# Another order around the second batch's attention, and v cast by ScalarE

## Chip, core and metric

The kernel runs on one core of a Trainium2 chip. The time is the device time of one launch in microseconds, lower is better. Batches and tiles are counted from 0 throughout, as in the code: "batch 1" is the second one.

## What is computed

Linear attention with cosine weights over 8 batches, 8 heads, 576 positions and 64 elements per head, and then a two-layer network with a leaky ReLU over the 4608 rows of 512 that it gives:

```python
def phi(x, c, s):
    r = np.maximum(x, 0.0)
    return np.concatenate([r * c, r * s], axis=-1)   # 64 -> 128
q_p, k_p = phi(q, cos_w, sin_w), phi(k, cos_w, sin_w)
kv  = np.einsum('bhsf,bhsd->bhfd', k_p, v)           # sum over positions
z   = np.sum(k_p, axis=2)
num = np.einsum('bhsf,bhfd->bhsd', q_p, kv)
den = np.einsum('bhsf,bhf->bhs', q_p, z)[..., None] + 1e-06
x   = (num / den)  # rows: batch and position, columns: head and element
h   = x @ w_in                                       # 512 -> 2048
out = np.maximum(0.01 * h, h) @ w_out                # 2048 -> 512
```

## The kernel before

**Tiling.** Of each batch's 576 positions 512 are its main part (four tiles of 128, j = 0 to 3) and 64 its tail. The tails of k and v join their own batch's sums (`kpt`, `vtail`); the tails of q of all batches form a ninth group of 512 rows, so that the network runs over 9 groups g of 512 rows each. Everything is cast to 16-bit floats before TensorE takes it, sums are in 32 bits in PSUM.

**Stages of a batch.** Loads of q, k and v (SyncE's queue; one pool `stage` of 7 buffers of 1 MB, handed out in order). `q_prep` and `k_main`/`k_tail` make phi on VectorE (some cosine halves on ScalarE). `v_main` and `v_tail` cast v. `kv_mm` does 4 x 9 matmuls for the sums over positions, with two columns of ones beside v, so that z comes along; `kv_all`, or `kv_half` for four heads, copies them out of PSUM on ScalarE. phi(q) is transposed, by TensorE for batches 0 and 1, by DMA from batch 2 on (`q_transpose_dma`). `num` (or `num_half`) multiplies by kv, `divide` on VectorE does den, its reciprocal and the product. The result is transposed to xT: TensorE and a copy by ScalarE for batches 0 to 2, DMA after that.

**The network.** `ffn1(g, m)` is a unit of four matmuls of 512 columns for one block m of 128 hidden features (16 of them); two blocks share a PSUM tile `h`, which ScalarE's Lrelu turns into `g`. `ffn2(g, i)` is a unit of four matmuls of the second product: tile i // 4 of 128 rows, a quarter of the hidden features each; the fourth unit of a tile is followed by the copy of `ps_o` to `osb` and the output DMA.

**PSUM.** 8 banks in three pools: "h" two tiles of two banks, "o" two tiles of one bank, "n" one tile of two banks. Each pool hands out its tiles in turn, so an allocation waits for the last reader of the tile that it takes over.

**Order.** It is written out by hand; each engine runs its instructions in the order of the program and waits on semaphores. Batch 1's attention stands between the last units of group 0's second product: this stretch runs at about 44 to 56 us of the profile. Behind it, a list of units (f1 and f2 alternating, 16 positions to a group) is woven with the steps of the later batches: each step has a position, and goes in front of the first unit whose position isn't smaller. `load_steps(b, pk, pv, pq)` gives the positions of the loads of k, v and q, `kv_steps(b, start, step, mm, eng_v)` those of phi(k), of v's casts (`start + 3 * step`) by engine `eng_v`, and of `kv_all` (`mm`); `q_steps(b, start, step, lag)` those of phi(q) and, `lag` later, of its transposition. All DMAs, loads, transpositions and outputs alike, are issued from SyncE's one queue in this order.

**The functions and lines that matter here:** L260 and L270 are the matmuls of `kv_mm`, L282 and L287 its copies, L368 and L333 those of num, L385 the transposes, L389 and L612 the copies to xT, L411 and L430 the two products, L419 the Lrelu, L228 and L230 the casts and copies (`copy`: ScalarE, and the other engines), L222 phi on VectorE, L86 and L96 the loads of main parts and tails, L304 and L315 the DMA transpositions, L446 the outputs.

Of the kernel before, what the change touches and what calls it, by code (L numbers as in the profile page):

```python
# [9 lines left out]
dt = mybir.dt  # L10
# [3 lines left out]
P = 128  # L14
J = 4
# [3 lines left out]
def kernel(  # L19
# [14 lines left out]
    nc = tc.nc  # L34
# [11 lines left out]
    NE = D + 2  # L46
# [3 lines left out]
    def pool(name, bufs, space=None):  # L50
        kw = {"space": space} if space is not None else {}
        return ctx.enter_context(tc.tile_pool(name=name, bufs=bufs, **kw))
# [16 lines left out]
    ps_o = pool("ps_o", 2, PS)  # L69
    ps_n = pool("ps_n", 1, PS)  # L70

    def psum(where, shape, dtype, name):
        p = {"h": ps_h, "o": ps_o, "n": ps_n}[where]
        return p.tile(shape, dtype, name=name, tag="ps_" + where)

    st = {}
    ACT, DVE, POOL = nc.scalar, nc.vector, nc.gpsimd
# [81 lines left out]
    def idle(n):  # L159
# [21 lines left out]
        base=0,  # L181
# [3 lines left out]
    for o in range(2):  # L185
# [3 lines left out]
            base=MAIN,  # L189
# [24 lines left out]
    kv = [const.tile([P, H, NE], dt.float16, name=f"kv{b}") for b in range(B)]  # L214
# [3 lines left out]
    def phi_half(eng, o, i, col):  # L218
        if eng is ACT:
            nc.scalar.activation(o, i, AF.Relu, scale=col)  # L220
        else:
            eng.tensor_scalar(  # L222
                out=o, in0=i, scalar1=0.0, scalar2=col, op0=ALU.max, op1=ALU.mult
            )
# [11 lines left out]
    def k_main(b, j, eng_c, eng_s, lo=0, hi=H):  # L236
        kpm, kst = st["kpm", b], st["k", b]
        for eng, t, f in ((eng_c, cos_t, 0), (eng_s, sin_t, D)):
            phi_half(
                eng, kpm[:, lo:hi, j, f : f + D], kst[:, lo:hi, j, :], t[:, j : j + 1]  # L240
            )
# [6 lines left out]
    def v_main(b, lo, hi, eng):  # L248
        copy(eng, vmain[b % 2][:, lo:hi, :, 0:D], st["v", b][:, lo:hi])
# [6 lines left out]
    def kv_mm(b, hg, ps):  # L256
        kpm, kpt = st["kpm", b], st["kpt", b]
        for cc in range(2):
            c = 2 * hg + cc
            nc.tensor.matmul(  # L260
                ps[:, 2 * cc * NE : 2 * (cc + 1) * NE],
                lhsT=kpt[:, c, :],
                rhs=vtail[b % 2][:, c].rearrange("p a e -> p (a e)"),
                start=True,
                stop=False,
            )
            for o in range(2):
                h = 2 * c + o
                for j in range(J):
                    nc.tensor.matmul(  # L270
                        ps[:, (2 * cc + o) * NE : (2 * cc + o + 1) * NE],
                        lhsT=kpm[:, h, j, :],
                        rhs=vmain[b % 2][:, h, j, :],
                        start=False,
                        stop=(o == 1 and j == J - 1),
                    )
# [4 lines left out]
            kv_mm(b, hg, ps[:, hg])  # L281
        nc.scalar.copy(kv[b].rearrange("p (a h) e -> p a (h e)", a=2), ps)  # L282

    def kv_half(b, hg, where):
        ps = psum(where, [P, 4 * NE], dt.float32, "ps_kvh")
        kv_mm(b, hg, ps)
        nc.scalar.copy(kv[b][:, 4 * hg : 4 * hg + 4].rearrange("p h e -> p (h e)"), ps)  # L287

    def q_src(g, j):
        if g < B:  # L290
# [84 lines left out]
    def x_transpose_half(g, jp, hg, ps=None, out=True):  # L375

        if ("xT", g) not in st:
            st["xT", g] = xtpool.tile([P, NKC, MAIN], dt.float16, name="xT")
        xp = st["xp", g, jp]
        if ps is None:  # L380
            ps = psum("o", [P, 2, 2 * P], dt.float16, "ps_xth")
        for cc in range(2):
            for o in range(2):
                h = 4 * hg + 2 * cc
                nc.tensor.transpose(  # L385
                    ps[:, cc, o * P : (o + 1) * P], xp[:, o, h : h + 2, :], ident
                )
        if out:
            nc.scalar.copy(  # L389
                st["xT", g][:, 2 * hg : 2 * hg + 2, jp * 2 * P : (jp + 1) * 2 * P], ps  # L390
            )
# [10 lines left out]
    def ffn1(g, m, lo=0, hi=MAIN, chunks=range(NKC), where="h"):  # L402

        if ("g", g) not in st:
            st["g", g] = gpool.tile([P, NFT, MAIN], dt.float16, name="g")
        if m % 2 == 0 and chunks[0] == 0 and lo == 0:
            st["h", m // 2] = psum(where, [P, 2, MAIN], dt.float32, "ps_h")
        xT = st["xT", g]
        ps = st["h", m // 2]
        for c in chunks:  # L410
            nc.tensor.matmul(  # L411
                ps[:, m % 2, lo:hi],
                lhsT=w1[m // 4][c // 2][:, c % 2, m % 4 : 512 : 4],
                rhs=xT[:, c, lo:hi],
                start=(c == 0 and lo == 0),
                stop=(c == NKC - 1 and hi == MAIN),
            )
        if m % 2 == 1 and chunks[-1] == NKC - 1 and hi == MAIN:
            nc.scalar.activation(st["g", g][:, m - 1 : m + 1, :], ps, AF.Lrelu)  # L419

    def ffn2(g, i, eng=DVE):
        tt, part = divmod(i, 4)
        if g == NG - 1 and tt == 3:
            last_tile(*divmod(part, 2))
            return
        if part == 0 and ("ps_o", g, tt) not in st:
            st["ps_o", g, tt] = psum("o", [P, DM], dt.float32, "ps_o")
        ps = st["ps_o", g, tt]
        for m in range(4 * part, 4 * part + 4):
            nc.tensor.matmul(  # L430
                ps,
                lhsT=st["g", g][:, m, tt * P : (tt + 1) * P],
                rhs=w2[:, m, :],
                start=(m == 0),
                stop=(m == NFT - 1),
            )
        if part == 3 and eng is not None:
            ffn2_out(g, tt, eng)

    def ffn2_out(g, tt, eng):  # L440
        ps = st["ps_o", g, tt]
        osb = opool.tile([P, DM], dt.float32, name="osb", tag="osb")
        if g < B:
            copy(eng, osb, ps)
            rows = out[g * S : g * S + MAIN, :].rearrange("(p j) d -> p j d", j=J)
            nc.sync.dma_start(rows[:, tt, :], osb)  # L446
            return
        copy(eng, osb, ps)
        for o in range(2):
            r0 = (2 * tt + o) * S + MAIN  # L450
            nc.sync.dma_start(out[r0 : r0 + TAIL, :], osb[o * TAIL : (o + 1) * TAIL, :])
# [100 lines left out]
            u()  # L552
        assert not steps

    def f1(g, m):
        return lambda: ffn1(g, m)

    def f2(g, i):
        return lambda: ffn2(g, i)
# [21 lines left out]
    ps = psum("n", [P, 2, DM], dt.float32, "ps_o")  # L581
# [11 lines left out]
        ffn2(0, 4 * tt + 3, None)  # L593
    ffn2_out(0, 2, DVE)
    ffn2_out(0, 3, DVE)
    kv_half(1, 0, "h")
    for j in range(J):
        k_main(1, j, ACT if j < 3 else DVE, DVE, 4, 8)
    v_main(1, 4, 6, POOL)
    v_main(1, 6, 8, ACT)  # L600
    ffn2(0, 2)
    num_half(1, 0, 0, "h")
    num_half(1, 1, 0, "n")
    ffn2(0, 4 + 2)
    kv_half(1, 1, "h")
    ffn2(0, 3, ACT)
    num_half(1, 0, 1, "h")
    num_half(1, 1, 1, "h")
    ps = psum("n", [P, 2, MAIN], dt.float16, "ps_x")
    for jp in range(2):  # L610
        x_transpose_half(1, jp, 0, ps[:, :, jp * 2 * P : (jp + 1) * 2 * P], False)
    nc.scalar.copy(st["xT", 1][:, 0:2, :], ps)  # L612
    ffn2(0, 4 + 3, ACT)
    for m in range(2):
        ffn1(1, m, 0, MAIN, range(0, 2))
    x_transpose_half(1, 0, 1)
    x_transpose_half(1, 1, 1, psum("n", [P, 2, 2 * P], dt.float16, "ps_xth"))
    for m in range(2, 4):
        ffn1(1, m, 0, MAIN, range(0, 2))
    for m in range(4):  # L620
# [3 lines left out]

    units = []
    for m in range(4, NFT):
        units.append((8 + m / 2, f1(1, m)))
    for g in range(1, NG):
        ahead = {1: 8, 2: 4}.get(g, 0)
        order = [f2(g, i) for i in range(ahead)]  # L630
# [10 lines left out]
    def kv_steps(b, start, step, mm, eng_v, n_act=0):  # L641
        at(start - 0.01, kp_tiles, b)
        at(start, k_tail, b, DVE, DVE)
        for i in range(J):
            at(start + (i + 1) * step, k_main, b, i, ACT if i < n_act else DVE, DVE)
        at(start + 3 * step, v_main, b, 0, 4, eng_v)
        at(start + 3 * step + 0.1, v_main, b, 4, 8, eng_v)
        at(start + 3 * step + 0.2, v_tail, b, eng_v)
        at(mm, kv_all, b)

    def load_steps(b, pk, pv, pq):
        at(pk, load_k, b)
        at(pv, load_v, b)
        at(pq, load_main, "q", q, b)
# [6 lines left out]
    def q_steps(b, start, step, lag):  # L661
        for j in range(J):
            at(start + j * step, q_prep, b, j)
            at(start + j * step + lag, q_transpose_dma, b, j)
# [9 lines left out]
    kv_steps(3, 20, 0.7, 24, ACT)  # L674
    out_steps(3, 24.5, 1.4, 1)

    load_steps(4, 20.5, 22.5, 19)
    kv_steps(4, 28, 1.2, 34, POOL)
    q_steps(4, 30, 1, 0.8)
    out_steps(4, 36.8, 2, 1.6)  # L680

    for b in range(5, NG):
        base = 16 * (b - 2)
        if b < B:
            load_steps(b, base - 14.5, base - 13, base - 17)
            kv_steps(b, base - 9.5, 1.4, base - 2, POOL)
        else:
            for j in range(J):
                at(base - 11.5 + 2 * j, load_qtail, j)
        q_steps(b, base - 8, 2, 1)  # L690
        out_steps(b, base + 1, 2, 1.6)
# [32 lines left out]
```

## Time and profile before

| what | value |
|---|---|
| median of 3 runs | 298.75 us (296.34, 298.75, 429.62) |
| profiled execution | 297.1 us, span 295.0 us |
| TensorE busy in the span | 286.8 us (97%) |
| VectorE, ScalarE, GpSimd busy | 132.9, 107.8, 24.0 us |
| granted TensorE clock, mean | 1.000 |
| matmuls of the two products | 592 + 560 instructions |
| DMA moved | 56.93 MB |

The span runs from the first to the last instruction that the profiler saw; the time includes what lies around it. Starts are in microseconds from the span's start. In a row of the timeline the first number is the start, the second the duration of what is merged in the row, and a bracket tells how long the engine had been idle and who released it. PE is TensorE, DVE VectorE, ACT ScalarE, POOL GpSimd, SPq the instruction queue of SyncE. The matmuls are pipelined and their ends are modelled, so that two rows overlap where TensorE is full, and the distance between starts tells more than the durations.

### The profile page before, as it was taken

How to read it: one execution, taken by the hardware profiler on the slowest of the kernel's cores; microseconds unless marked ns; L12 is line 12 of the kernel's file. 1: busy time of each engine (PE TensorE's matmuls, PEld its weight loads, DVE VectorE, ACT ScalarE, POOL GpSimd, SP SyncE). 2: the span in 40 equal slices, each digit the busy share in tenths (PEclk: the TensorE clock that was granted, in tenths of full speed). 3: DMA queues.
4: the chain of work that ended last, by engine and by line, in shares of the span. 5: the costliest groups of instructions: out<-in, count | busy, mean ns of one | idle time of the engine just before them, and what ended most of it. 6: DMA issues, size and time to landing. Idle time of an engine off the chain costs nothing.

```text
span 295.0 us, 4811 instructions
## 1 busy us (share of the span) xinstructions
PE 286.8 (97%) x1932; PEld 153.9 (52%) x1932; DVE 132.9 (45%) x328; ACT 107.8 (37%) x128; POOL 24.0 (8%) x36
## 2 busy tenths in 40 slices
PE   8799999999999999999999999999999999999995
PEld 3575556465455455555545554555445544444444
DVE  6950578934855925933572347333323211000011
ACT  4846376664253422242223222322222232222200
POOL 2055000000000400400300021000000000000000
PEclk9999999999999999999999999999999999999999
DMA  7999999999999999999978995416681210011132
GB/s 219 355 386 406 290 350 346 329 170 333 186 269 285 205 248 265 267 158 315 241 143 230 216 234 126 110 53 144 143 159 56 71 53 38 36 43 61 41 71 71
DMA packets 88773, 56.93 MB, mean 193 GB/s; under 512 B 56880, under 2 KB 81712, under 8 KB 88240
## 3 DMA queue, kind: packets, MB, share of 16 engines
q1 hardware_dynamic: 88672, 56.57, 75.7%
q8 instruction: 15, 0.25, 0.4%
q14 instruction: 6, 0.05, 0.1%
q10 hardware_dynamic: 80, 0.07, 0.1%
HBM read 36.70 MB, written 9.44 MB: 156 GB/s over the span
## 4 chain that ended last, share of the span: by engine, by line
PE 80%; DMA 13%; SPq 3%; ACT 1%; issue 0%; DVE 0%; POOL 0%
PE ps_h L411 37%; PE ps_o L430 37%; DMA ktl<-in_k_dram 5%; DMA w1st<-in_moe_w_in_dram 4%; DMA vst<-in_v_dram 3%; PE ps_num L333 3%; PE ps_kv L270 2%; SPq L86 2%; SPq L96 1%; SPq L138 1%; DMA out_dram<-osb 1%; PE ps_kv L260 0%; ACT xT L389 0%; ACT g L419 0%; ACT xT L612 0%
## 5 line engine op out<-in xcount | busy, mean ns | idle before, releaser
L411 PE MATMUL ps_h<-xT,w 128*128 128x512 f16 (+1 forms) x592 | 143.1, 373 | 0.6 <-ACT g L419 0.2
L430 PE MATMUL ps_o<-w,g 128*128 128x512 f16 x560 | 139.4, 379 | 0.0
L419 ACT ACTIVATE g<-ps_h 128x1024 f16<-128x1024 f32 x72 | 73.5, 1024 | 141.7 <-PE ps_h L411 141.6
L411 PEld LDWEIGHTS <-w 128*128 128x128 f16 x592 | 64.3, 114 | 53.6 <-issue 1.3
L430 PEld LDWEIGHTS <-g 128*128 128x128 f16 x560 | 54.1, 98 | 61.6 <-issue 0.2
L230 DVE COPY osb<-ps_o 128x512 f32<-128x512 f32 x33 | 22.7, 690 | 76.6 <-PE ps_o L430 76.6
L344 DVE TENSOR_SCALAR den<-ps_num 128x8 f32<-128x8 f32 x28 | 4.6, 166 | 54.1 <-PE ps_num L333 54.1
L230 POOL CAST vmain<-vst 128x1024 f16<-128x1024 f32 (+1 forms) x9 | 9.8, 1107 | 136.6 <-DMA vst<-in_v_dram 136.6
L349 DVE TENSOR_TENSOR xs<-ps_num,rden 128x512 f16<-128x512 f32 x28 | 19.4, 691 | 1.0
L222 DVE TENSOR_SCALAR kpm<-kst,sin_t 128x512 f16<-128x512 f32 (+1 forms) x40 | 18.3, 472 | 0.7 <-DMA kst<-in_k_dram 0.7
L222 DVE TENSOR_SCALAR qp<-qst,cos_t 128x512 f16<-128x512 f32 (+1 forms) x34 | 16.3, 479 | 3.8 <-DMA qst<-in_q_dram 3.8
L222 DVE TENSOR_SCALAR qp<-qst,sin_t 128x512 f16<-128x512 f32 (+1 forms) x34 | 16.1, 472 | 0.0
L333 PEld LDWEIGHTS <-qpT 128*128 128x128 f16 (+1 forms) x256 | 11.2, 101 | 7.3 <-issue 1.9
L222 DVE TENSOR_SCALAR kpm<-kst,cos_t 128x512 f16<-128x512 f32 (+1 forms) x29 | 14.1, 485 | 0.1
L333 PE MATMUL ps_num<-kv,qpT 128*128 128x66 f16 (+1 forms) x256 | 12.4, 194 | 0.0
L270 PEld LDWEIGHTS <-kpm 128*128 128x128 f16 x256 | 10.6, 97 | 2.8 <-DVE kpm L222 0.7
L162 PE MATMUL ps_idle<-blank 128*128 128x512 f16 x28 | 9.2, 467 | 1.2 <-DVE blank L157 1.2
L228 ACT COPY qpT<-ps_qt 128x1024 f16<-128x1024 f16 x8 | 7.8, 1019 | 7.0 <-PE ps_qt L323 7.0
L230 DVE CAST w<-w2st 128x2048 f16<-128x2048 f32 x4 | 4.9, 1227 | 11.7 <-DMA w2st<-in_moe_w_out_dram 11.7
L230 POOL CAST w<-w1st 128x1024 f16<-128x1024 f32 x8 | 8.3, 1042 | 16.4 <-DMA w1st<-in_moe_w_in_dram 16.4
L270 PE MATMUL ps_kv<-vmain,kpm 128*128 128x66 f16 x192 | 8.1, 193 | 0.0
L348 DVE RECIPROCAL rden<-den 128x8 f32<-128x8 f32 x36 | 7.3, 203 | 1.2
(57 smaller groups left out, 102.6 us busy)
## 6 DMA issues: line engine op xcount, KB each, us to landing
out_dram<-osb SPq DMA_DIRECT2D x32, 256.0 KB, 2.7
qst<-in_q_dram SPq DMA_DIRECT2D x7, 1024.0 KB, 8.0
kst<-in_k_dram SPq DMA_DIRECT2D x6, 1024.0 KB, 7.9
vst<-in_v_dram SPq DMA_DIRECT2D x6, 1024.0 KB, 8.3
w1st<-in_moe_w_in_dram SPq DMA_DIRECT2D x8, 512.0 KB, 12.1
w2st<-in_moe_w_out_dram SPq DMA_DIRECT2D x4, 1024.0 KB, 11.3
kst<-in_k_dram SPq DMA_DIRECT2D x4, 512.0 KB, 8.2
vst<-in_v_dram SPq DMA_DIRECT2D x4, 512.0 KB, 8.6
```

Of the source, the lines that this page charges most:

```text
L86: nc.sync.dma_start(st[nm, b][:, lo:hi], src[b, lo:hi, 0:MAIN, :].rearrange("h (p j) d -> p h j d", j=J),)
L162: nc.tensor.matmul(ps, lhsT=blank[:, 0:P], rhs=blank)
L222: eng.tensor_scalar(out=o, in0=i, scalar1=0.0, scalar2=col, op0=ALU.max, op1=ALU.mult)
L228: nc.scalar.copy(o, i)
L230: eng.tensor_copy(o, i)
L270: nc.tensor.matmul(ps[:, (2 * cc + o) * NE : (2 * cc + o + 1) * NE], lhsT=kpm[:, h, j, :], rhs=vmain[b % 2][:, h, j, :], start=False, stop ...
L333: nc.tensor.matmul(ps[lo:hi, h // 4, (h % 4) * NE : (h % 4 + 1) * NE], lhsT=qpT[:, h, lo:hi], rhs=kv[b][:, h, :],)
L348: nc.vector.reciprocal(rden, den)
L349: nc.vector.tensor_tensor(out=xs, in0=ps[:, :, 0 : 4 * NE].rearrange("p a (b e) -> p a b e", e=NE)[:, :, :, 0:D], in1=rden.rearrange("p (a ...
L411: nc.tensor.matmul(ps[:, m % 2, lo:hi], lhsT=w1[m // 4][c // 2][:, c % 2, m % 4 : 512 : 4], rhs=xT[:, c, lo:hi], start=(c == 0 and lo == 0 ...
L419: nc.scalar.activation(st["g", g][:, m - 1 : m + 1, :], ps, AF.Lrelu)
L430: nc.tensor.matmul(ps, lhsT=st["g", g][:, m, tt * P : (tt + 1) * P], rhs=w2[:, m, :], start=(m == 0), stop=(m == NFT - 1),)
```

## The change

Between the last units of group 0's second product and the first units of group 1, the same work is put in another order: `ffn2(0, 2)` goes ahead of `kv_half(1, 0)`, whose copy now follows the first pair of phi(k) casts; `ffn2(0, 6)` and `ffn2(0, 3)` go ahead of where they were; the last unit of tile (0, 1) is split into two pairs of matmuls (`ffn2_mm`), one ahead of the second num pair and one behind the first transposes. The output copy of tile (0, 0) follows `kv_half(1, 1)`, that of tile (0, 1) goes to VectorE. The two last transposes share a PSUM tile of pool "o" and stand on either side of the first `ffn1` units; h of m = 4 and 5 goes to pool "n". For batches 4 to 7 v is cast by ScalarE instead of GpSimd, q is loaded just ahead of k, for batch 4 k is loaded somewhat later too, and phi(q) of batch 4 is spaced by 0.8 positions instead of 1.

```diff
--- before.py
+++ after.py
@@ -281,10 +281,16 @@
             kv_mm(b, hg, ps[:, hg])
         nc.scalar.copy(kv[b].rearrange("p (a h) e -> p a (h e)", a=2), ps)
 
-    def kv_half(b, hg, where):
-        ps = psum(where, [P, 4 * NE], dt.float32, "ps_kvh")
-        kv_mm(b, hg, ps)
-        nc.scalar.copy(kv[b][:, 4 * hg : 4 * hg + 4].rearrange("p h e -> p (h e)"), ps)
+    def kv_half(b, hg, where, out=True):
+        st["kvh", hg] = psum(where, [P, 4 * NE], dt.float32, "ps_kvh")
+        kv_mm(b, hg, st["kvh", hg])
+        if out:
+            kv_half_out(b, hg)
+
+    def kv_half_out(b, hg):
+        nc.scalar.copy(
+            kv[b][:, 4 * hg : 4 * hg + 4].rearrange("p h e -> p (h e)"), st["kvh", hg]
+        )
 
     def q_src(g, j):
         if g < B:
@@ -425,17 +431,19 @@
             return
         if part == 0 and ("ps_o", g, tt) not in st:
             st["ps_o", g, tt] = psum("o", [P, DM], dt.float32, "ps_o")
-        ps = st["ps_o", g, tt]
-        for m in range(4 * part, 4 * part + 4):
+        ffn2_mm(g, tt, 4 * part, 4 * part + 4)
+        if part == 3 and eng is not None:
+            ffn2_out(g, tt, eng)
+
+    def ffn2_mm(g, tt, lo, hi):
+        for m in range(lo, hi):
             nc.tensor.matmul(
-                ps,
+                st["ps_o", g, tt],
                 lhsT=st["g", g][:, m, tt * P : (tt + 1) * P],
                 rhs=w2[:, m, :],
                 start=(m == 0),
                 stop=(m == NFT - 1),
             )
-        if part == 3 and eng is not None:
-            ffn2_out(g, tt, eng)
 
     def ffn2_out(g, tt, eng):
         ps = st["ps_o", g, tt]
@@ -552,8 +560,8 @@
             u()
         assert not steps
 
-    def f1(g, m):
-        return lambda: ffn1(g, m)
+    def f1(g, m, where="h"):
+        return lambda: ffn1(g, m, where=where)
 
     def f2(g, i):
         return lambda: ffn2(g, i)
@@ -593,28 +601,34 @@
         ffn2(0, 4 * tt + 3, None)
     ffn2_out(0, 2, DVE)
     ffn2_out(0, 3, DVE)
-    kv_half(1, 0, "h")
-    for j in range(J):
+    ffn2(0, 2)
+    kv_half(1, 0, "h", False)
+    k_main(1, 0, ACT, DVE, 4, 8)
+    kv_half_out(1, 0)
+    for j in range(1, J):
         k_main(1, j, ACT if j < 3 else DVE, DVE, 4, 8)
     v_main(1, 4, 6, POOL)
     v_main(1, 6, 8, ACT)
-    ffn2(0, 2)
+    ffn2(0, 4 + 2)
     num_half(1, 0, 0, "h")
     num_half(1, 1, 0, "n")
-    ffn2(0, 4 + 2)
+    ffn2(0, 3, None)
     kv_half(1, 1, "h")
-    ffn2(0, 3, ACT)
+    ffn2_out(0, 0, ACT)
+    ffn2_mm(0, 1, 12, 14)
     num_half(1, 0, 1, "h")
     num_half(1, 1, 1, "h")
     ps = psum("n", [P, 2, MAIN], dt.float16, "ps_x")
     for jp in range(2):
         x_transpose_half(1, jp, 0, ps[:, :, jp * 2 * P : (jp + 1) * 2 * P], False)
     nc.scalar.copy(st["xT", 1][:, 0:2, :], ps)
-    ffn2(0, 4 + 3, ACT)
+    ffn2_mm(0, 1, 14, 16)
+    ffn2_out(0, 1, DVE)
+    ps = psum("o", [P, 2, 2, 2 * P], dt.float16, "ps_x1")
+    x_transpose_half(1, 0, 1, ps[:, 0])
     for m in range(2):
         ffn1(1, m, 0, MAIN, range(0, 2))
-    x_transpose_half(1, 0, 1)
-    x_transpose_half(1, 1, 1, psum("n", [P, 2, 2 * P], dt.float16, "ps_xth"))
+    x_transpose_half(1, 1, 1, ps[:, 1])
     for m in range(2, 4):
         ffn1(1, m, 0, MAIN, range(0, 2))
     for m in range(4):
@@ -624,7 +638,7 @@
 
     units = []
     for m in range(4, NFT):
-        units.append((8 + m / 2, f1(1, m)))
+        units.append((8 + m / 2, f1(1, m, "n" if m < 6 else "h")))
     for g in range(1, NG):
         ahead = {1: 8, 2: 4}.get(g, 0)
         order = [f2(g, i) for i in range(ahead)]
@@ -674,16 +688,16 @@
     kv_steps(3, 20, 0.7, 24, ACT)
     out_steps(3, 24.5, 1.4, 1)
 
-    load_steps(4, 20.5, 22.5, 19)
-    kv_steps(4, 28, 1.2, 34, POOL)
-    q_steps(4, 30, 1, 0.8)
+    load_steps(4, 21.4, 22.5, 21.3)
+    kv_steps(4, 28, 1.2, 34, ACT)
+    q_steps(4, 30, 0.8, 0.8)
     out_steps(4, 36.8, 2, 1.6)
 
     for b in range(5, NG):
         base = 16 * (b - 2)
         if b < B:
-            load_steps(b, base - 14.5, base - 13, base - 17)
-            kv_steps(b, base - 9.5, 1.4, base - 2, POOL)
+            load_steps(b, base - 14.5, base - 13, base - 14.6)
+            kv_steps(b, base - 9.5, 1.4, base - 2, ACT)
         else:
             for j in range(J):
                 at(base - 11.5 + 2 * j, load_qtail, j)
```

## Prediction

> **What bounds the kernel now.** I read the page first, then the waits, then TensorE's timeline where it is not full, then the other engines around each place that the change touches. Batches are counted from 0, so "batch 1" is the second and "batch 4" the first whose v cast changes engine.
>
> ```profile
> span 295.0 us, 4811 instructions
> PE 286.8 (97%) x1932; PEld 153.9 (52%) x1932; DVE 132.9 (45%) x328; ACT 107.8 (37%) x128; POOL 24.0 (8%) x36
> PEclk9999999999999999999999999999999999999999
> ```
>
> TensorE has work nearly throughout, at full granted clock. The busy share alone would hide small bubbles, since ends of matmuls are modelled, so I take starts: four 512-column matmuls in a row take 0.86 us wherever nothing waits (0.86 x4 all along the chain that ended last). What is over that is lost. TensorE's timeline:
>
> ```profile
> 44.40 0.22 PE L260 MATMUL ps_kvh<-vtail,kpt 128*128 128x132 f16 x1
> 44.90 0.41 PE L270 MATMUL ps_kvh<-vmain,kpm 128*128 128x66 f16 x8 [0.28 <-DVE vmain L230]
> ...
> 47.70 0.22 PE L260 MATMUL ps_kvh<-vtail,kpt 128*128 128x132 f16 x1
> 48.13 0.58 PE L270 MATMUL ps_kvh<-vmain,kpm 128*128 128x66 f16 x8 [0.21 <-POOL vmain L230]
> ...
> 50.68 1.03 PE L430 MATMUL ps_o<-w,g 128*128 128x512 f16 x4
> 51.94 1.02 PE L411 MATMUL ps_h<-xT,w 128*128 128x512 f16 x4 [0.24 <-ACT xT L612]
> ...
> 53.25 2.99 PE L411 MATMUL ps_h<-xT,w 128*128 128x512 f16 x12
> 56.48 5.34 PE L411 MATMUL ps_h<-xT,w 128*128 128x512 f16 x24 [0.25 <-ACT g L419]
> ```
>
> A 132-column start is followed 0.06 us later by the next elsewhere: 0.44 lost at 44.40, 0.37 at 47.70; the eight short matmuls at 48.13 need 0.42 to the next group instead of 0.26, so 0.16 more. 50.68 + 0.86 = 51.54, the next starts 51.94: 0.40. 53.25 + 12 x 0.216 = 55.84, the next starts 56.48: 0.64 (0.24 inside the row, 0.41 behind it). Together **2.0 us**. From 56.48 to the last matmuls I find only about 0.75 us more, around 221 to 234, in the tail group that the change leaves alone. So all that the reorder can win is 2.0 us of 297; two per cent, about what a measurement of this kernel can tell from no change, is 6 us.
>
> **The change, part by part.** The order of batch 1, followed from 44.40:
>
> - ffn2(0, 2) goes ahead of kv_half(1, 0): TensorE reaches kv at 44.40 + 0.86 = 45.26, VectorE's v cast ends 44.85 and ScalarE's 45.13. The 0.44 is covered. ScalarE now casts cosine of j = 0 ahead of kv's copy; that cast can't start before k's second half lands (45.94 now). So 45.94 + 0.44, then 0.38 for the copy: 46.76. TensorE is there at 45.26 + 0.63 + 0.86 = 46.75; with 0.05 for the signal (51.89 to 51.94 above) it loses 0.06.
> - ffn2(0, 3) goes ahead of kv_half(1, 1): num takes 0.51, ffn2 0.86, so kv starts at 48.18. POOL's cast ends 47.46 + 0.62 = 48.08, ScalarE's at about 48.2 and is needed only by the second half. The 0.37 and 0.16 are covered.
> - Between kv_half(1, 1) and num there are now two matmuls (0.43) where there were four. kv ends 48.81, its copy starts 0.22 later and takes 0.38; num can start at 49.45, TensorE is there at 49.24. A **new wait of 0.21**, and up to 0.16 for starting short matmuls again (as at 48.13): 0.1.
> - The other two matmuls and half a transposition now cover the 1.01 us copy of xT. Four heads' transposes end 50.47; the copy runs about 50.67 to 51.68. But x_transpose_half(1, 0, 1) needs VectorE's division: den at about 49.95, then 0.17, 0.20, 0.69 with their gaps, 51.08. TensorE is there at 50.90 and loses 0.3; after 0.22 of transposing it is at 51.43 and waits 0.3 for xT, where it waited 0.40.
> - The last transposition stands alone, so its copy (0.55) ends at about 53.55, before the chunks that need it (53.68): the 0.24 is gone. h of m = 4 and 5 goes to the bank pair "n", free since 51.68: the 0.41 is gone.
>
> Sum: -2.01 + 0.06 + 0.21 + 0.1 + 0.3 + 0.3 = **-1.0** (between -2.0, no new wait, and +0.5, each new wait three times as long with the old ones gone).
>
> What is late next: the output copy of (0, 1) moves from ScalarE to VectorE, which issues one each 0.64 us (1.28 for the two at 44.76) and has no idle time from 50.17 to 60.25. It starts 0.17 earlier, so batch 2's last kpm comes at 60.25 + 0.47 = 60.72, and TensorE comes to kv_all(2) at 61.66 - 1.04 = 60.62, needing that piece four weight loads later. I take **+0.2** (0 to 0.5).
>
> **v on ScalarE** from batch 4. The nearest rows are batch 3, which already has it:
>
> ```profile
> 79.76 1.02 ACT L419 ACTIVATE g<-ps_h 128x1024 f16<-128x1024 f32 x1 [4.65 <-PE ps_h L411]
> 80.68 1.98 ACT L228 CAST vmain<-vst 128x1024 f16<-128x1024 f32 x2
> 82.57 0.83 ACT L228 CAST vtail<-vtl 64x256 f16<-64x256 f32 x2
> 83.42 1.03 ACT L419 ACTIVATE g<-ps_h 128x1024 f16<-128x1024 f32 x1
> ```
>
> From the start of g to the end of the last v cast: 83.40 - 79.76 = 3.64. For batch 4 the casts' positions (31.6 to 31.8) lie behind the last f1 unit of batch 2 (31.5), so they follow its g, and only four f2 units lie between that and kv_all(4):
>
> ```profile
> 100.10 1.03 ACT L419 ACTIVATE g<-ps_h 128x1024 f16<-128x1024 f32 x1 [0.70 <-PE ps_h L411]
> 102.96 0.48 DVE L222 TENSOR_SCALAR kpm<-kst,sin_t 128x512 f16<-128x512 f32 x1
> 103.36 0.22 PE L260 MATMUL ps_kv<-vtail,kpt 128*128 128x132 f16 x1
> ```
>
> 100.10 + 3.64 + 0.05 = 103.79 against 103.36: TensorE waits 0.43, whatever the shift before it, since both follow the same f1. With a slow restart **+0.5** (0 to 1.0). Behind the casts stand kv's copy and the next g; for batches 5 to 7 kv_all comes three positions (over 5 us) later, and a g held 0.4 us is needed only some 4 us on: nothing. By "TensorE: Matmul & The Clock Gate" (the Trainium skill, on the array's architecture) ScalarE and VectorE take their queues strictly in order, so that these casts can't step aside; the row at 83.42, a g starting just as v's cast ends, agrees, and an engine that could reorder would give 0 in place of 0.5.
>
> POOL's casts are gone, and with them this:
>
> ```profile
> 97.16 2.55 POOL L230 CAST vmain<-vst 128x1024 f16<-128x1024 f32 x2 [49.08 <-DMA vst<-in_v_dram]
> 97.55 1.26 DVE L222 TENSOR_SCALAR kpm<-kst,cos_t 128x512 f16<-128x512 f32 x1
> 98.73 1.25 DVE L222 TENSOR_SCALAR kpm<-kst,sin_t 128x512 f16<-128x512 f32 x1
> ```
>
> Two casts of 1.26 instead of 0.48 and two of 0.6: 1.9 us less on VectorE. Without that, kpm of batch 4 (103.44 at its end, against TensorE's load at 103.36) would hold TensorE the moment it comes earlier. Eight pairs of 0.79 from 95.1 end at 101.4, TensorE comes at 102.5: 1.1 us of cover. "SBUF — State Buffer" (the Trainium skill, on who interferes with whom) says that VectorE in a two-port mode and GpSimd lock each other out for a whole instruction; the 1.26 beside a cast of 1.27 agrees, and by it the gain here is full.
>
> **Loads.** q of batch 4 goes from position 19 to 21.3, k from 20.5 to 21.4: behind all four transpositions of qp of batch 3 (18.8 to 21.2), not among them. SyncE's queue now:
>
> ```profile
> 77.60 0.52 SPq L86 DMA_DIRECT2D qst<-in_q_dram  x1
> 79.27 6.76 SPq L304 DMA_TRANSPOSE qpT<-qp  x2
> 86.08 0.57 SPq L86 DMA_DIRECT2D kst<-in_k_dram  x1
> 90.80 0.59 SPq L86 DMA_DIRECT2D vst<-in_v_dram  x1
> ```
>
> The transpositions took 2.5 to 3.5 each behind 1 MB of q; elsewhere 1.25. Three at 1.25 from about 78.2 put q and k at 82 to 83, k no later than its 86.08, landing 7.9 later (median) plus about 3 for the q ahead of it: 93. VectorE wants it at 92.9. At 3.3 each, q goes at 88 and k lands near 99. I take 0 (0 to +4.4). qp's transposes come sooner, which the last num of batch 3 needs. For batches 5 to 7 q goes just ahead of k; for batch 5 VectorE already waits 2.67 us for ktl (at 115.33) and TensorE loses nothing by it.
>
> **Sum**: -1.0 + 0.2 + 0.5 + 0 = -0.3. The profiled execution took 297.1 (span 295.0): **296.8**. The median shown, 298.75, is of runs at 296.34, 298.75 and one far off; 297.1 lies between the two near ones, so execution noise (2.4 us) is larger than the whole effect.
>
> **Rivals.** (1) The casts of batch 4 cost nothing and the reorder holds: 297.1 - 0.8 = 296.3. Against it stands the 3.64 measured. (2) The reorder only trades waits: two matmuls of cover (0.43) are less than the copies they stand for (0.60 for kv with its signal, 1.01 for xT), and the 1.0 is lost again; 297.1 + 0.5 = 297.6. For it: three of the new waits hang on VectorE and ScalarE chains that are already full. (3) The slower side: **k of batch 4 lands late**. VectorE, in order, sits at kpt; behind it are batch 3's last division and eight pairs, 7.9 us, then kv_all(4). It holds TensorE from a landing at about 94.6 on and makes the kernel slower than before from about 95.4; landing at 99 gives 99 + 7.9 = 106.9 against 102.5: 4.4, so 297.1 - 0.8 + 4.4 = 300.7, and halfway 298.5. For it: ktl already held VectorE 2.67 us for batch 5 at 115.33; against: nothing big is now in the ring ahead of the transposes.
>
> **How the numbers follow.** Forecast 0.45, (1) 0.2, (2) 0.15, (3) 0.17, the rest elsewhere. All lie within 6 us of 297, so within 2% gets 0.95; slower 0.04, for (3) with more behind it; faster 0.01, as only 2.0 us of bubbles are there. The range takes (1) and (2) with the noise of about 1.5 below and above, and half of (3): 294.6 to 299.6.
>
> **What would show it.** Right: TensorE's first matmul of f1 (1, 4) near 55.4 (now 56.48), small waits of num on kv's copy and of f1 on xT, about 0.4 at kv_all(4) on ScalarE's vtail, kpm of batch 4 at 0.48 throughout, POOL idle after 48.1. Wrong: TensorE idle over 1 us anywhere behind 62, kpt of batch 4 waiting for ktl, or f1 (1, 4) not before 56.3.

## The result, and the profile after

The changed kernel takes 295.85 us (median of 22 runs, 295.25 to 296.72), the kernel before 296.5 us (22 runs). The ratio of their undisturbed runs (two of the kernel before, at 302.96 and 429.62 us, are left out of it) is 0.997, with a 95% interval of 0.9957 to 0.9984: a gain of 0.5 to 1.3 us, well inside 2%. The forecast was 296.8 in a range of 294.6 to 299.6, a gain of 0.3.

The page of the changed kernel, its first lines:

```profile
span 294.7 us, 4802 instructions
PE 286.4 (97%) x1932; PEld 153.9 (52%) x1932; DVE 129.9 (44%) x329; ACT 117.9 (40%) x143; POOL 11.0 (4%) x20
```

GpSimd gave up 13 us of casts, ScalarE took on 10, VectorE is busy 3 us less: and the span is 0.3 us shorter. These totals explain nothing. What counts is where TensorE's starts are further apart than its work. Its timeline in batch 1, after:

```profile
45.48 0.22 PE L260 MATMUL ps_kvh<-vtail,kpt 128*128 128x132 f16 x1
...
48.34 0.22 PE L260 MATMUL ps_kvh<-vtail,kpt 128*128 128x132 f16 x1
48.40 0.52 PE L270 MATMUL ps_kvh<-vmain,kpm 128*128 128x66 f16 x8
48.75 0.22 PE L260 MATMUL ps_kvh<-vtail,kpt 128*128 128x132 f16 x1
...
49.06 0.59 PE L440 MATMUL ps_o<-w,g 128*128 128x512 f16 x2
49.69 0.67 PE L374 MATMUL ps_numh<-kv,qpT 128*128 128x66 f16 x16
...
50.65 0.59 PE L440 MATMUL ps_o<-w,g 128*128 128x512 f16 x2
51.33 0.40 PE L391 MATMUL ps_x<-ident,xp 128*128 128x128 f16 x4
51.91 1.02 PE L417 MATMUL ps_h<-xT,w 128*128 128x512 f16 x4 [0.18 <-ACT xT L624]
...
52.99 7.93 PE L417 MATMUL ps_h<-xT,w 128*128 128x512 f16 x36
```

Lost now: 0.09 at 48.40 (0.35 to the next group instead of 0.26), 0.20 (49.06 + 0.43 to 49.69), 0.25 (51.08 to 51.33), 0.34 at the wait for xT; nothing in front of either kv, and the 36 matmuls from 52.99 run without a break. That is 0.89 us where 2.01 were lost: **1.12 us gained**. The 1.12 compares these two executions; the old order lost less in another one (below, the casts, loads and spacing alone). The start at 45.48 instead of the 45.26 foretold comes from before the changed stretch, where TensorE waited for the cast of w2 until 42.90.

Some 57 us later, at kv_all(4), TensorE and ScalarE:

```profile
99.01 3.62 PE L440 MATMUL ps_o<-w,g 128*128 128x512 f16 x16
103.03 0.22 PE L260 MATMUL ps_kv<-vtail,kpt 128*128 128x132 f16 x1 [0.41 <-ACT vtail L228]
```

```profile
99.21 1.02 ACT L425 ACTIVATE g<-ps_h 128x1024 f16<-128x1024 f32 x1 [0.70 <-PE ps_h L417]
100.26 1.99 ACT L228 CAST vmain<-vst 128x1024 f16<-128x1024 f32 x2
102.16 0.82 ACT L228 CAST vtail<-vtl 64x256 f16<-64x256 f32 x2
```

Sixteen matmuls from 99.01 end at 102.47; kv starts 103.03, as v's last cast ends at 102.98. **0.57 us are given back**, at the place foretold. Between this and the tail group at 220 no further start is late by 0.1 us. Net 1.12 - 0.57 = 0.55 us by the lost starts of the two profiles, 0.65 by the medians; the spans differ by 0.3 because batch 1 starts 0.22 later in the profile after (45.48, not 45.26).

### The profile page after: what moved, and what is told of

It reads as the page before. It is cut to its first block, busy times and chain, and to the rows that moved or that the text cites. A ratio compares the mean times of both kernels' runs of the same rounds, so it can differ in the third digit from the quotient of the medians.

```text
span 294.7 us, 4802 instructions
## 1 busy us (share of the span) xinstructions
PE 286.4 (97%) x1932; PEld 153.9 (52%) x1932; DVE 129.9 (44%) x329; ACT 117.9 (40%) x143; POOL 11.0 (4%) x20
## 4 chain that ended last, share of the span: by engine, by line
PE 81%; DMA 8%; SPq 6%; ACT 1%; issue 1%; DVE 1%; ACTq 0%
PE ps_h L417 38%; PE ps_o L440 37%; SPq L96 4%; DMA w2st<-in_moe_w_out_dram 4%; DMA w1st<-in_moe_w_in_dram 4%; PE ps_num L339 3%; PE ps_kv L270 2%; SPq L86 1%; DMA out_dram<-osb 1%; SPq L138 1%; ACT vmain L228 1%; SPq L142 1%; PE ps_kv L260 1%; DVE w L230 0%; PE ps_numh L374 0%
## 5 line engine op out<-in xcount | busy, mean ns | idle before, releaser
L230 DVE COPY osb<-ps_o 128x512 f32<-128x512 f32 x34 | 23.4, 690 | 80.1 <-PE ps_o L440 80.1
L222 DVE TENSOR_SCALAR kpm<-kst,sin_t 128x512 f16<-128x512 f32 (+1 forms) x40 | 16.5, 428 | 0.8 <-DMA kst<-in_k_dram 0.8
L222 DVE TENSOR_SCALAR kpm<-kst,cos_t 128x512 f16<-128x512 f32 (+1 forms) x29 | 13.0, 449 | 0.1
L228 ACT CAST vmain<-vst 128x1024 f16<-128x1024 f32 (+1 forms) x14 | 12.9, 953 | 0.4 <-DMA vst<-in_v_dram 0.3
```

Source lines behind the costliest of these rows:

```text
L222: eng.tensor_scalar(out=o, in0=i, scalar1=0.0, scalar2=col, op0=ALU.max, op1=ALU.mult)
L228: nc.scalar.copy(o, i)
L230: eng.tensor_copy(o, i)
```

## Experiments

Each variant was profiled, and those whose time matters were also timed in alternation with the kernel before. The sums of TensorE's lost starts are read as above; they are steadier than the span, because the loads of the first 45 us shift every execution's batch 1 by up to 1.1 us (kv_half(1, 1) starts between 47.30 and 48.42 in the profiles with the new order).

**The order alone** (casts and positions of loads and phi(q) as before):

```diff
-    load_steps(4, 21.4, 22.5, 21.3)
-    kv_steps(4, 28, 1.2, 34, ACT)
-    q_steps(4, 30, 0.8, 0.8)
+    load_steps(4, 20.5, 22.5, 19)
+    kv_steps(4, 28, 1.2, 34, POOL)
+    q_steps(4, 30, 1, 0.8)
...
-            load_steps(b, base - 14.5, base - 13, base - 14.6)
-            kv_steps(b, base - 9.5, 1.4, base - 2, ACT)
+            load_steps(b, base - 14.5, base - 13, base - 17)
+            kv_steps(b, base - 9.5, 1.4, base - 2, POOL)
```

> Only the new order in batch 1; casts of v, loads and phi(q) positions as before. Theory A (as in the prediction: kpm of batch 4, slowed by GpSimd, would hold TensorE as soon as it comes earlier): f1 (1, 4) starts about 1.0 us earlier, but kv_all(4) waits 0.8 to 1.0 us on VectorE, net 0 to 0.2 us, ratio 0.9995. Theory B (VectorE's chain starts with a division that TensorE releases, so both come earlier together; but the last transposed phi(q) of batch 3 lands at an unchanged 93.9): num (3, 3) waits about 0.6 us for it, kv_all(4) nothing, net 0.4 us, ratio 0.9985. Theory C (nothing downstream is late): the whole 1.0, ratio 0.9965.

Ratio 0.9954 (0.9937 to 0.9972). That is a gain of 0.8 to 1.9 us. Batch 1 loses the same 0.89 us, and nothing is lost behind it up to the tail group. Theory C holds; A, a statement of the prediction, falls. VectorE's rows show why:

```profile
93.42 0.17 DVE L350 TENSOR_SCALAR den<-ps_num 128x8 f32<-128x8 f32 x1 [0.59 <-PE ps_num L339]
...
97.23 1.26 DVE L222 TENSOR_SCALAR qp<-qst,sin_t 128x512 f16<-128x512 f32 x1
98.42 1.25 DVE L222 TENSOR_SCALAR kpm<-kst,cos_t 128x512 f16<-128x512 f32 x1
...
101.46 0.48 DVE L222 TENSOR_SCALAR kpm<-kst,sin_t 128x512 f16<-128x512 f32 x1
```

The casts are stretched as before, but the chain starts with a division that TensorE releases (93.42, before 94.92). TensorE earlier means VectorE earlier, and kpm is as just-in-time as it was: it ends at 101.94, and kv starts at 101.86 and needs it a few weight loads later (103.44 and 103.36 before).

**The casts, loads and spacing alone** (batch 1 in the old order):

> Only the casts of v on ScalarE and the new positions of loads and phi(q); batch 1 in the order of before. Theory (a wait of 0.57 us at kv_all(4) is all that this part does to TensorE): 0.5 us slower than the kernel before, ratio 1.002, TensorE's rows in batch 1 as before. Rival (freeing VectorE of GpSimd's casts gains by itself): no wait or a gain, ratio 1.000 or below.

Ratio 0.9998 (0.9984 to 1.0012). The wait at kv_all(4) is there (0.57, on ScalarE's vtail), so the mechanism is as expected; the time is not 1.002. In this execution the first half of v was already cast when TensorE came to batch 1, so the 0.44 is missing, the second kv costs 0.33 instead of 0.53, 0.10 is lost ahead of the transposes, and in all 1.48 us are lost, not 2.01. So the loss of the old order is not a fixed number: it depends on how the loads fall. That this accounts for the time of all 12 runs is not shown, as only one was profiled. The time of this variant doesn't settle the size of that part; the runs below do it by the waits.

**v of batch 4 on GpSimd again** (two expectations for the same kernel, the second one made after the run of the order alone):

```diff
-    kv_steps(4, 28, 1.2, 34, ACT)
+    kv_steps(4, 28, 1.2, 34, POOL)
```

> The changed kernel with v of batch 4 alone cast by GpSimd again. Theory (the cast on ScalarE costs TensorE 0.57 us at kv_all(4), but GpSimd's cast would slow VectorE): the wait on ScalarE goes, VectorE's kpm casts beside GpSimd's take 1.26 us again, kpm of batch 4 ends near 103.4 instead of 101.5 and TensorE waits about 0.85 us for it at kv_all(4): 0 to 0.4 us slower than the changed kernel, ratio to the kernel before 0.997 to 0.999. Rival (VectorE's slowing is off the path): no wait at kv_all(4), 0.5 us faster than the changed kernel, ratio 0.995.

> The same kernel as in the run with v of batch 4 on GpSimd, for a profile. Theory: no wait on ScalarE at kv_all(4); of VectorE's casts ahead of it four are stretched (1.26 and 0.6 us), so that kpm of batch 4, now behind all four phi(q), ends near 103.4 and TensorE waits about 0.8 us. Rival: VectorE is done in time, as it just was in the run of the order alone, and TensorE waits 0.

Ratio 0.9976 (0.9961 to 0.9992), not faster than the changed kernel. TensorE now waits for the other engine:

```profile
101.41 0.22 PE L260 MATMUL ps_kv<-vtail,kpt 128*128 128x132 f16 x1
101.46 0.26 PE L270 MATMUL ps_kv<-vmain,kpm 128*128 128x66 f16 x3
102.34 0.33 PE L270 MATMUL ps_kv<-vmain,kpm 128*128 128x66 f16 x5 [0.62 <-DVE kpm L222]
```

Three short matmuls and then 0.78 us lost, on the fourth j, as kpm ends at 102.28. VectorE's two casts beside GpSimd's (95.14 to 97.37) take 1.26 and 1.25 us again:

```profile
95.20 1.26 DVE L222 TENSOR_SCALAR qp<-qst,sin_t 128x512 f16<-128x512 f32 x1
96.39 1.25 DVE L222 TENSOR_SCALAR kpm<-kst,cos_t 128x512 f16<-128x512 f32 x1
...
101.80 0.48 DVE L222 TENSOR_SCALAR kpm<-kst,sin_t 128x512 f16<-128x512 f32 x1
```

The lock between VectorE and GpSimd that the Trainium skill describes ("SBUF — State Buffer", who interferes with whom) fits these rows. The same slowed casts cost TensorE nothing in the order alone, and 0.78 us here. The difference is the spacing of phi(q): 0.8 positions instead of 1 put all four of its pairs ahead of the last kpm.

**The spacing by itself**, on top of the order alone:

```diff
-    q_steps(4, 30, 1, 0.8)
+    q_steps(4, 30, 0.8, 0.8)
```

> The order alone (casts of v on GpSimd and loads in their positions of before), and phi(q) of batch 4 spaced by 0.8 positions instead of 1. Theory (the spacing is what makes the other two changes necessary: it puts one more pair of casts ahead of the last kpm and one more transposition ahead of k of batch 5): TensorE waits 0.7 to 0.9 us for kpm at kv_all(4); the wait at num (4, 2) is covered by that delay or stays under 0.6. Rival (the spacing does nothing): no wait over 0.1 us behind 62 us, as in the order alone.

297.36 us in one run, where the order alone has a median of 295.4. Three waits appear behind 62 us: 0.78 at kv_all(4), 0.76 at num (4, 2) and 0.38 at kv_all(5). The first is as expected; the second is larger than expected, and the third was not expected. The second comes by a chain of its own, seen on SyncE's queue, VectorE and TensorE:

```profile
100.97 6.74 SPq L310 DMA_TRANSPOSE qpT<-qp  x3
107.76 0.57 SPq L86 DMA_DIRECT2D kst<-in_k_dram  x1
```

```profile
115.29 0.35 DVE L222 TENSOR_SCALAR kpt<-ktl,cos_t 128x256 f16<-128x256 f32 x1 [3.51 <-DMA ktl<-in_k_dram]
```

```profile
117.09 0.41 PE L339 MATMUL ps_num<-kv,qpT 128*128 128x66 f16 x8 [0.60 <-DVE xs L355]
```

The closer spacing brings a third transposition ahead of k of batch 5 in the one queue (two in the order alone). k's tail lands later, VectorE stands at kpt for 3.51 us (2.58 in the order alone), and the division behind it is late. The next num waits for that division, because it takes over the PSUM tile that the division reads.

**The old positions of the loads** in the changed kernel:

```diff
-    load_steps(4, 21.4, 22.5, 21.3)
+    load_steps(4, 20.5, 22.5, 19)
...
-            load_steps(b, base - 14.5, base - 13, base - 14.6)
+            load_steps(b, base - 14.5, base - 13, base - 17)
```

> The changed kernel with the loads of q and k (batches 4 to 7) in their positions of before. Theory (the positions do nothing for TensorE, as the order alone ran without a wait behind 62 us): the wait at kv_all(4) stays 0.57, no other wait over 0.1 behind 62 us, span within 0.3 us of what its start gives. Rival (transposed phi(q) of batch 3 or k of batch 4 would now come late): a wait of 0.3 us or more at num (3, 3).

The theory fails: besides the 0.57 a wait of 0.61 us comes at num (4, 2), one batch later than the rival had it.

```profile
116.35 0.42 PE L339 MATMUL ps_num<-kv,qpT 128*128 128x66 f16 x8 [0.45 <-DVE xs L355]
```

It is the same chain (kpt waits 3.35 us for ktl). In the changed kernel q of batch 5 comes behind the transpositions:

```profile
98.91 5.37 SPq L310 DMA_TRANSPOSE qpT<-qp  x4
104.38 0.53 SPq L86 DMA_DIRECT2D qst<-in_q_dram  x1
104.97 0.63 SPq L86 DMA_DIRECT2D kst<-in_k_dram  x1
```

They take about 1.3 us each, k goes out at 104.97 instead of 107.45, and kpt waits 2.15. Counted from the start of kv_half(1, 1), kpt begins 66.1 us later there and 67.3 here. So in these two executions the new positions are worth 0.6 us, given the new spacing; neither was repeated, and the last run below shows that the new positions don't always cover this wait.

**Cover for the casts at kv_all(4)**, in two ways. The casts of v's tail on VectorE instead of ScalarE:

```diff
-    def kv_steps(b, start, step, mm, eng_v, n_act=0):
+    def kv_steps(b, start, step, mm, eng_v, n_act=0, eng_t=None):
...
-        at(start + 3 * step + 0.2, v_tail, b, eng_v)
+        at(start + 3 * step + 0.2, v_tail, b, eng_t or eng_v)
...
-    kv_steps(4, 28, 1.2, 34, ACT)
+    kv_steps(4, 28, 1.2, 34, ACT, 0, DVE)
```

> The changed kernel with the two small casts of batch 4's v tail on VectorE instead of ScalarE, in the same place of the order. Theory (0.57 us at kv_all(4) are two casts too many in ScalarE's queue): ScalarE is done at about 102.3, VectorE at 102.1, TensorE comes at 102.5, so the wait falls from 0.57 to at most 0.1: 0.5 us faster than the changed kernel, ratio to the kernel before 0.995. Rival (the wait is for something else, such as VectorE, which is only masked): the wait stays above 0.4 us and the time as it is, 0.997.

Ratio 0.9948 (0.9927 to 0.9968); the wait is 0. And kv_all(4) two units later (two expectations for the same kernel):

```diff
-    kv_steps(4, 28, 1.2, 34, ACT)
+    kv_steps(4, 28, 1.2, 35, ACT)
```

> The changed kernel with kv_all(4) two units later (position 35 instead of 34), casts on ScalarE as they are. Theory (TensorE only lacks 0.57 us of cover for ScalarE's casts): two more units, 1.73 us, cover them, the wait is 0, no other appears, 0.57 us off the span from batch 1 on. Rival (the wait moves on, to num (4, 0) on kv's copy or to the next Lrelu): a wait of 0.3 us or more within the next 10 us.

> The same kernel as in the one look at kv_all(4) two units later, now timed. Theory: the changed kernel's time less 0.57 us, ratio to the kernel before 0.995. Rival: as the changed kernel, 0.997.

The wait is 0 here too, and none takes its place; ratio 0.9946 (0.9926 to 0.9965). **One number in the order removes the whole price of the casts.** Both variants are faster than the kernel before. Against the changed kernel they lose 0.57 us less at kv_all(4), and their medians (295.03 and 295.31 us) are lower, but the intervals of the ratios overlap with its 0.9957 to 0.9984. They can't be told from each other or from the order alone.

**h of m = 4 and 5 in the old pool:**

```diff
-        units.append((8 + m / 2, f1(1, m, "n" if m < 6 else "h")))
+        units.append((8 + m / 2, f1(1, m)))
```

> The changed kernel with h of m = 4 and 5 of batch 1 in pool h again. Theory: f1 (1, 4) waits for ScalarE's Lrelu of m = 0 and 1, about 0.41 us, as before; everything else as in the changed kernel. Rival (the wait of before went because the copy to xT comes earlier, not because of the other bank): no wait, 0.

```profile
52.29 2.75 PE L417 MATMUL ps_h<-xT,w 128*128 128x512 f16 x12
55.29 2.97 PE L417 MATMUL ps_h<-xT,w 128*128 128x512 f16 x13 [0.25 <-ACT g L425]
```

52.29 + 12 x 0.216 = 54.88, the next starts 55.29: the 0.41 is back, to the hundredth. The other pool is what removed it.

**Two tries at the 0.89 us left in batch 1.** First, on the order alone, the copy to xT in halves and the first products in halves:

```diff
-    ps = psum("n", [P, 2, MAIN], dt.float16, "ps_x")
+    ps = psum("n", [P, 2, 2, MAIN], dt.float16, "ps_x")
     for jp in range(2):
-        x_transpose_half(1, jp, 0, ps[:, :, jp * 2 * P : (jp + 1) * 2 * P], False)
-    nc.scalar.copy(st["xT", 1][:, 0:2, :], ps)
+        x_transpose_half(1, jp, 0, ps[:, jp, :, 0 : 2 * P])
...
+    for m in range(2):
+        ffn1(1, m, 0, half, range(0, 2))
     ps = psum("o", [P, 2, 2, 2 * P], dt.float16, "ps_x1")
     x_transpose_half(1, 0, 1, ps[:, 0])
     for m in range(2):
-        ffn1(1, m, 0, MAIN, range(0, 2))
+        ffn1(1, m, half, MAIN, range(0, 2))
```

> The order alone (casts and loads as before), and in it the first copy to xT in two halves, each in a bank of its own, and the first ffn1 units of batch 1 in halves of 256 columns, the first half ahead of x_transpose_half(1, 0, 1). Theory: of the waits of 0.25 (division) and 0.34 (copy to xT) about 0.17 is left, 0.4 us less than the order alone, ratio to the kernel before 0.994. Rival (the chain of division and copy just shows up later, at the chunks 2 and 3): the same as the order alone, 0.9955.

Ratio 0.999 (0.9968 to 1.0012): worse than the order alone. 1.42 us are lost in batch 1 instead of 0.89, and the waits name it:

```profile
PE ps_x L391 <- ACT xT L395: 0.9, 2, 0.7
```

```profile
49.56 0.39 PE L391 MATMUL ps_x<-ident,xp 128*128 128x128 f16 x4
50.62 0.38 PE L391 MATMUL ps_x<-ident,xp 128*128 128x128 f16 x4 [0.67 <-ACT xT L395]
```

The first wait costs 0.84 us from start to start: the transposes of the second half wait for the copy of the first, though they write another bank. The two halves belong to one tile, and the wait seems to be set for the tile (in the next run, with a tile for each, it is gone). The second wait, 0.40 us, is the same between the halves of the tile in pool "o". Second, a tile for each quarter, with kv_all(4) at 35 and kv_all(2) a unit later:

```diff
+    x_transpose_half(1, 0, 0, psum("n", [P, 2, 2 * P], dt.float16, "ps_x0"))
+    x_transpose_half(1, 1, 0, psum("o", [P, 2, 2 * P], dt.float16, "ps_x1"))
...
-    kv_steps(2, 9.7, 0.5, 13, DVE, 2)
+    kv_steps(2, 9.7, 0.5, 13.4, DVE, 2)
     for j in range(J):
-        at(13.5 + 1.1 * j, num, 2, j)
-        at(14.8 + 1.1 * j, x_transpose, 2, j, "o" if j < 2 else "h")
+        at(13.9 + 1.05 * j, num, 2, j)
+        at(15 + j, x_transpose, 2, j, "o" if j < 2 else "h")
...
-    kv_steps(4, 28, 1.2, 34, ACT)
+    kv_steps(4, 28, 1.2, 35, ACT)
```

> The changed kernel, with kv_all(4) at position 35, and in batch 1 every transposed quarter of x in a PSUM tile of its own (pools n, o, n, n), the first ffn1 units in halves as in the run with halves, and kv_all(2) and what follows it a unit later, since VectorE's chain would be late for it. Theory (a wait goes once no tile is shared with a copy that still reads, and the cover is there): of 0.20 + 0.25 + 0.34 + 0.57 us about 0.4 is left, 0.9 to 1.0 us less than the changed kernel, 1.5 to 2.0 less than the kernel before, ratio 0.9935 to 0.995. Rival (the chain of ScalarE and VectorE in batch 1 is full, so that every wait taken away comes back at the chunks 2 and 3, at kv_all(2) or at a Lrelu): only the 0.57 is gained, ratio 0.996.

Ratio 0.9971 (0.996 to 0.9983). Batch 1 now loses 0.54, and kv_all(4) nothing. But two new waits of 0.52 stand behind it:

```profile
72.39 0.40 PE L403 MATMUL ps_xt<-ident,xs 128*128 128x128 f16 x4 [0.36 <-DVE xs L355]
```

```profile
116.89 0.41 PE L339 MATMUL ps_num<-kv,qpT 128*128 128x66 f16 x8 [0.36 <-DVE xs L355]
```

The first is put down to my own shift of batch 2's steps (a transpose too close behind its division); no run tests that by itself. The second is again kpt of batch 5, which waited 3.27 us for ktl. TensorE comes to this num 0.5 us earlier than in the changed kernel (due at 116.37, not 116.88), but kpt starts 0.6 us later (115.09, not 114.48), though the load went out within 0.1 us of the same time. In the run with kv_all(4) at 35 TensorE came just as early, at 116.39, kpt started at 114.55, and there was no wait. So part of these 0.52 us is how the load fell in this one execution.

## Why the prediction was right, and where it was not

- **The bound** was right: 2.0 us of bubbles in batch 1, a full TensorE behind them, so the result had to be small. What batch 1 gained reached the end of the span but for the wait at kv_all(4). But 2.0 is the sum of one execution; the old order lost 1.48 in the other one that was profiled.
- **The new order**: -1.0 foretold, -1.12 read. Of the new waits 0.06, 0.21, 0.1, 0.3 and 0.3 were expected, and 0, 0.20, 0, 0.25 and 0.34 came. The 0.44, 0.24 and 0.41 went, and of the 0.53 at the second kv 0.09 is left, where the prediction had it covered; the 0.1 that it put on num's restart didn't come. So the sum of the terms fits partly by luck: 0.1 was foretold in one place and 0.09 came in another. The run with the old pool shows the 0.41 by itself.
- **kv_all(2)**: +0.2 foretold, 0 came. VectorE's last kpm ended at 60.82 (60.72 foretold), and kv started at 60.77, but its matmul that needs that piece, the fourth of the first head, started at 60.92. This term was mis-sized, and by the prediction's own figures: 60.62 + 0.06 + 3 x 0.03 = 60.77 is later than 60.72, which gives 0.
- **The casts**: +0.5 foretold, 0.57 read. From g's start to the end of v's last cast took 3.77 us, not the 3.64 of batch 3. ScalarE's rows at 99.21, 100.26 and 102.16 stand in program order, as the sum needs it. The Trainium skill ("TensorE: Matmul & The Clock Gate", the array's architecture), from which the prediction took that ScalarE's queue is strictly in order, agrees with these rows.
- **VectorE without GpSimd's casts**: kpm ended at 101.49 (101.4 foretold). The statement that kpm beside GpSimd's casts "would hold TensorE the moment it comes earlier" was wrong as put; both move together. It holds only with the closer spacing, as the order alone (0) and the spacing (0.78) show.
- **The loads** were put at 0 with a bad end of +4.4. q and k of batch 4 went out at 82.48 and 83.08, within the forecast, and kpt didn't wait. But their worth was not 0: beside the new spacing, 0.61 us more are lost without the new positions, at batch 5, where the prediction took a wait of VectorE that cost nothing before to be harmless.
- **The level**: the profiled execution, 297.1, was about 0.6 above the median that more runs give (296.5). So 296.8 and 295.85 differ more by their base than by the effect, -0.3 against -0.65. The noise of 2.4 us that the prediction set against the effect was that of single runs; the medians of 22 runs each tell the effect from none. The ends of the range follow only roughly from the 1.5 us that it names (296.3 - 1.5 = 294.8 and 297.6 + 1.5 = 299.1, where it has 294.6 and 299.6).

What stays open is the exact split in time between the parts: ratios of 0.9946 to 0.9954 with intervals of 0.0035 to 0.0041 don't rank the three best variants, and the loss by the casts and loads alone was not to be seen in its time.

## What to carry to other kernels

When one engine is full, read how far apart its starts are, and follow each bubble to the instruction that ends last; a reorder can win that sum and no more. A change of several parts can contain one that costs (here the spacing of phi(q), 1.9 us of waits by itself) and others that repair it, so that those others look useful when one of them is undone, while together all three cost 0.57 us of waits against the order alone: try each part alone, and not only by undoing it. When a stage comes earlier, ask of each thing downstream whether its chain starts at that stage, and comes earlier with it, or at a load, and stays.

## What was not expected of the hardware and the program

GpSimd's slowing of VectorE hits whichever casts run at that moment (in batch 4 two took 1.25 to 1.26 us and two 0.61 to 0.62, instead of 0.48), and cost TensorE between 0 and 0.78 us by what stood behind them. Transpositions by DMA took 1.25 us of SyncE's queue each when no load was ahead of them in it and 6.74 us for three behind 1 MB of q. And in this program two halves of one PSUM tile in different banks were kept apart as if they were one place: TensorE stood idle for 0.67 us at the first of them.
